# Up-projection of eight token tiles by seven products of half blocks

## The chip, the cores and the metric

The kernel runs on one core of a Trainium2 chip. The metric is the device time of one execution in microseconds (us); a kernel's time is the median of several executions. Engines are named as in the profile: PE is the matrix engine (PEld its weight loads), DVE is VectorE, ACT is ScalarE, POOL is GpSimd, SP is the engine that issues most transfers.

## The reference

A transformer block of 2048 tokens of width 640: linear attention with 32 heads behind a layer norm, then a feed-forward part behind another. Cut to what is computed:

```
def _A_ref(x, wqkv, w_phi, wo):                  # 32 heads of 20
    q, k, v = split_heads(x @ wqkv)
    pq, pk = q @ w_phi, k @ w_phi
    phi_q = concat(softmax(pq), softmax(-pq));  phi_k = concat(softmax(pk), softmax(-pk))
    kv = sum_s(phi_k v);  z = sum_s(phi_k)
    o = (phi_q kv) / (phi_q z + 1e-6)
    return o @ wo
def _B_ref(x, w1, w2):                           # w1 640 x 1728, w2 1728 x 640
    return silu(x @ w1) @ w2
h  = x + _A_ref(layernorm(x), wqkv, w_phi, wo)
h2 = h + _B_ref(layernorm(h), w1, w2)
```

## The kernel before

The 2048 tokens are 16 tiles of 128. Weights and activations stay in SBUF in bf16; PE writes into PSUM, 8 banks of 512 fp32 values per partition, and each result is taken out of its bank by ACT or DVE. The work of each tile goes through these steps, whose names are those of the order: keys and values (`K`, `V`, `ex`, `su`, `rk`, `sc`, `ve`, `kv`), queries (`Q`, `qe`, `qs`, `qr`, `qt`), attention (`D` on PE, `E` on DVE, `ot` a transposing transfer), output projection (`G{t}0`, `G{t}1` on PE, ten matmuls of 320 columns in all), residual (`ga`, DVE, line 856), second layer norm (`lm`, `ls`, `hn` on ACT, `lr` on POOL, `ht` a transposing transfer into `HnT`).

The feed-forward part works on units of tiles: (0, 1), (2 to 5), (6 to 9), (10 to 13), (14, 15). For a unit starting at tile a, the step `u{a}.{f}` makes one 128-wide block of the 1728 hidden columns (`ffn_up`, line 931): five matmuls, one for each 128-row chunk of the 640 inputs, that stream 512 columns (4 tiles) into one bank. There are 13 such blocks, f = 0 to 12, and `u{a}.L` makes the last 64 columns. `s{a}.{f}` is the SiLU on ACT (`ffn_silu`, line 954), from the bank into `shT`. In the units of two tiles a block streams 256 columns, and two blocks share a bank.

The down-projection already works on pairs of tiles by seven products of half blocks: `T1` to `T4` are sums of the halves of w2 on DVE (line 1001), `S1.t` to `S4.t` sums of the hidden rows (DVE, line 1018), `p1.t` to `p7.t` the products, seven matmuls of 320 columns each (line 1036), `r1`, `r2`, `r3`, `r7` take a bank with the residual into an fp32 tile (DVE, line 1044), and `w11` to `w22` add a bank to it and give the output rows (DVE, line 1051).

The order of all steps is written out by hand as one list, `ORDER`; each engine runs its own steps in the order of the list, and semaphores hold a step back until its inputs are there and its tile or bank is free. Banks are handed out by a ring (`ps_half`, `ps_two`): the next bank is the one handed out longest ago, and a matmul into it waits until its last reader has ended.

At the start PE runs matmuls of constants (`warm`), transposes the key weights (`wk`) and folds them (`fk{c}`, line 345), transposes the first normalised tiles (`xt`, line 530), and makes the first values chunk by chunk (`V0.{c}`, line 583) and the first keys (`K0.{c}`).

Of the kernel before, what the change touches and what calls it, by code (L numbers as in the profile page):

```python
# [27 lines left out]
ve9 sc5 xn12 kv5 sc6 rk7 ex8 wq5 st13 K9 fq5 sc7 ones6 ex9 load7 xt10 kv6 rs14 ref10 xn11 rs13 fq5e su8
Q0 kv7 st15 su9 eqr0 rk8 K10 qe0 V10 xn13 sc8 Q1 xn14 rs15 ex10 qs0 xt12 V12 kv8 ve10 rk9 sc9 ref13 qe1
su10 load9 ql0 ve12 load3 qs1 rk10 sc10 xt11 ref12 kv9 ref11 xt13 K12 xn15 K11 ex12 su12 K13 load1 ex11  # L30
ex13 load10 V11 kv10 xt14 su11 K14 ql1 load4 qi0 ve11 eqr1 V13 rk11 eqp su13 qi1 rk12 sc11 kv11 qr1
ref14 xt15 rk13 qr0 sc12 K15 ex14 su14 load0 Q2 ve13 kv12 sc13 ref15 ex15 rk14 su15 qe2 V14 rk15 V15
ve14 load5 Q3 kv13 sc14 mask1 kv14 ve15 sc15 qt1 qs2 load2 kv15 bd0 Q7 qt0 ql2 load6 load8 qi2 Q5 qe3
halves bd1 D0 D1 qr2 qe7 qe5 Q4 qs3 ql3 E0 Q10 E1 qi3 qr3 qs5 qe4 qe10 qt2 Q6 ql5 D2 ot0 qs4 qe6 ot1 Q9
qi5 ql4 qi4 qr5 qt3 qt5 E2 G00 qe9 G01 ga0 lm0 qr4 G11 ot2 G10 ls0 Q11 lr0 D3 qs6 qe11 Q8 ga1 E3 lm1 qt4
hn0 qs7 ot3 D5 E5 ls1 Q13 G20 qe8 lr1 ht0 G21 hn1 qe13 Q14 ht1 ga2 Q15 qr6 qs8 qe14 Q12 G31 qe15 qr7 D4
G30 qr8 E4 ot5 qt6 qe12 u0.L padL0 T3.0 u0.4 ga3 u0.6 qs9 s0.L G50 G51 D6 T1.1 T1.2 ga5 lm2 s0.4 s0.6
ls2 qt7 lm5 T2.2 u0.0 u0.8 s0.0 T3.2 ot4 s0.8 D7 lr2 lm3 E6 u0.12 ls5 qt8 u0.2 s0.2 padL1 E7 T4.2 S3.0
G41 ls3 T1.0 ot6 T3.1 lr5 G40 u0.10 D8 ga4 p7.0 T2.1 E8 G61 hn2 ot7 T2.0 lt0 hn5 lr3 lm4 s0.12 T4.1 G60
# [4 lines left out]
u2.11 qs14 E11 s2.8 s2.11 G90 S3.2 ls8 G91 D12 p7.2 qr14 G101 ga9 hn6 r7.2 S1.2 lm9 lr7 p1.2 qt13 ot11
D13 ls9 E12 S2.2 G100 lr9 lr8 hn7 p2.2 r1.2 qt14 p6.2 ga10 G110 w11.2 r2.2 p4.2 hn9 ht6 ot12 ht9 G111
ht7 E13 S3.4 D14 hn8 w21.2 S4.2 ga11 p5.2 w22.2 p7.4 lm11 ht8 r3.2 lm10 E14 ot13 ls10 S1.4 p1.4 r7.4
p3.2 r1.4 out0 S2.4 out1 G121 u6.L G120 p6.4 qs15 u6.8 ga12 G131 ot14 r2.4 p5.4 s6.8 qr15 lm12 ls11 G130
p4.4 w21.4 lr10 u6.12 ga13 out3 qt15 lr11 w22.4 out5 s6.12 u6.5 w12.2 G140 ls12 r3.4 D15 s6.L u6.4 lt6
hn10 lr12 ht10 hn11 G141 u6.0 ga14 E15 lm13 ls13 u6.11 s6.5 p2.4 s6.11 hn12 s6.4 u6.7 u6.10 u6.9 u6.2
s6.10 s6.2 u6.6 ot15 s6.0 s6.7 w11.4 lr13 G151 hn13 u6.3 s6.6 S4.4 ht11 ht12 s6.9 s6.3 G150 u6.1 ht13  # L50
p3.4 u10.L s6.1 S3.6 lm14 u10.7 ga15 u10.12 p7.6 s10.7 S3.8 S1.6 s10.L lt10 lm15 w12.4 ls14 u10.0 u10.2
p1.6 r1.6 u10.4 ls15 s10.2 out2 s10.12 u10.6 lr14 lr15 r7.6 hn15 hn14 S2.6 p6.6 S4.6 ht15 p2.6 s10.0
p4.6 r2.6 p3.6 p5.6 ht14 w21.6 u10.8 s10.4 r3.6 u10.3 u10.1 w22.6 w11.6 u14.L p7.8 s10.8 s10.3 w12.6
out4 s10.6 S1.8 r7.8 p1.8 u14.0 u10.10 u10.5 r1.8 s10.5 s14.L s10.1 out6 S2.8 p6.8 S4.8 u10.11 r2.8 p5.8
S3.10 u10.9 s10.9 p4.8 s10.11 w21.8 p2.8 u14.10 s14.0 w22.8 s10.10 r3.8 p3.8 p7.10 w11.8 u14.4 S1.10
u14.2 p2.10 p1.10 out7 S2.10 s14.2 w12.8 r7.10 s14.10 p4.10 u14.12 r1.10 p6.10 S4.10 u14.8 S3.12 s14.4
r2.10 w21.10 p5.10 S1.12 u14.6 p1.12 out9 w11.10 p3.10 S2.12 p2.12 r3.10 r1.12 s14.8 out8 w11.12 p6.12
p7.12 w22.10 r2.12 r7.12 s14.6 lt14 p5.12 S3.14 out11 S4.12 p1.14 s14.12 S1.14 p4.12 S2.14 r1.14 w12.10
w21.12 w22.12 p3.12 r3.12 p7.14 r7.14 p6.14 r2.14 S4.14 p4.14 w12.12 p5.14 out10 p3.14 p2.14 p2.14x
w21.14 w22.14 out13 out12 r3.14 out15 w12.14 w11.14 w11.14x out140 out141 out142  # L60
""".split()


# [1 line left out]
def kernel(  # L65
# [14 lines left out]
    T = 16  # L80
# [30 lines left out]
    keys = proj_ctx.enter_context(tc.tile_pool(name="keys", bufs=1, side="right"))  # L111
    proj = proj_ctx.enter_context(tc.tile_pool(name="proj", bufs=1, side="right"))
    fold_ctx = ctx.enter_context(ExitStack())
    early = fold_ctx.enter_context(tc.tile_pool(name="fold", bufs=1))
    pools = {"att": None, "late": None}

# [109 lines left out]
    def add(name, emit):  # L226
        steps[name] = emit
# [719 lines left out]
    def rows_of(u):  # L947
        if u not in shT:
            shT[u] = pools["late"].tile([P, 4 * FC * P], BF16, name="shT", bufs=NSH)
        return shT[u]  # L950

    def ffn_silu(u, f0, f1):
        n = (u[1] - u[0]) * P
        nc.scalar.activation(  # L954
            rows_of(u)[:, f0 * n : f1 * n], ps_of.pop(("u", u, f0))[:, 0 : (f1 - f0) * n], AF.Silu
        )

    SHL = {}
# [100 lines left out]
    for t in PAIRS:  # L1059
# [45 lines left out]

# [29 lines left out]
```

## Time and profile before

| | us |
|---|---|
| median of 3 executions | 225.18 (224.81 to 225.22) |
| profiled execution, its own time | 225.49 |
| its span in the profile | 223.8 |
| PE busy | 218.2 (98%) |
| DVE busy | 173.0 (77%) |
| ACT busy | 144.4 (65%) |
| POOL busy | 70.2 (31%) |
| granted PE clock, mean | 0.998 of full speed |

The profile gives for each engine the union of the times in which an instruction of it ran; "mean ns" is the duration of one instruction, which overlaps its neighbours. Times in the trace count from the start of the span; the execution's own time is 1.7 us longer than the span.

### The profile page before, as it was taken

Reading aid. Unit: us, or ns where it says so; the run is one execution under the profiler, and the core shown is the slowest. Engines: PE = TensorE matmul, PEld = TensorE weight load, DVE = VectorE, ACT = ScalarE, POOL = GpSimd, SP = SyncE. Lnnn points to the kernel's source line nnn. Section 1 sums busy time; section 2 is a strip of 40 time slices with the busy share of each in tenths; the row PEclk is TensorE's granted clock in tenths of the full one; section 3 lists DMA queues with packets and bytes.
Section 4 is the critical chain, followed back from the end, with each engine's and each line's share of the span. In section 5 each row is a group of like instructions: output and inputs, shape, how many; then the busy total and the mean of one; then the engine's idle time right before and its main releaser. Section 6 shows DMA issues by size and latency. Waiting matters only on the chain.

```text
span 223.8 us, 5031 instructions
## 1 busy us (share of the span) xinstructions
PE 218.2 (98%) x1926; PEld 154.8 (69%) x1935; DVE 173.0 (77%) x305; ACT 144.4 (65%) x321; POOL 70.2 (31%) x136
## 2 busy tenths in 40 slices
PE   8799999999999999999999999999999999999994
PEld 5677777777777777887655577665455656778773
DVE  4899999999989999999999999944024344436694
ACT  2799999999979899997086774268568332321000
POOL 6789899899000130163020130132004000000000
PEclk9999999999999999999999999999999999999999
DMA  6994639679999874935536666434512410010012
GB/s 174 320 263 134 114 77 165 185 190 161 315 201 175 175 134 81 213 56 107 126 78 139 126 145 124 120 95 81 63 29 53 91 60 0 29 44 0 29 62 88
DMA packets 68158, 26.98 MB, mean 121 GB/s; under 512 B 61159, under 2 KB 67111, under 8 KB 68007
## 3 DMA queue, kind: packets, MB, share of 16 engines
q1 hardware_dynamic: 67335, 26.61, 53.3%
q8 instruction: 15, 0.25, 0.5%
q10 hardware_dynamic: 800, 0.06, 0.3%
q14 instruction: 8, 0.07, 0.1%
HBM read 9.55 MB, written 2.62 MB: 54 GB/s over the span
## 4 chain that ended last, share of the span: by engine, by line
PE 94%; DMA 2%; SPq 2%; issue 0%; DVE 0%
PE banks L931 25%; PE banks L1036 24%; PE banks L571 18%; PE banks L849 10%; PE banks L609 9%; PE banks L817 3%; PE banks L662 2%; DMA Wv<-in_A_wqkv_dram 2%; PE banks L942 1%; SPq L181 1%; PE banks L583 1%; PE banks L437 1%; PE banks L598 1%; SPq L178 1%; PE banks L530 0%
## 5 line engine op out<-in xcount | busy, mean ns | idle before, releaser
L931 PE MATMUL banks<-HnT,w_sb 128*128 128x512 bf16 (+1 forms) x316 | 60.0, 335 | 0.4
L954 ACT ACTIVATE shT<-banks 128x512 bf16<-128x512 f32 (+1 forms) x53 | 29.1, 586 | 45.8 <-PE banks L931 44.8
L931 PEld LDWEIGHTS <-w_sb 128*128 128x128 bf16 x325 | 31.2, 98 | 21.2
L571 PEld LDWEIGHTS <-XnT 128*128 128x128 bf16 x300 | 28.5, 98 | 9.5
L494 POOL TENSOR_SCALAR xn<-X,mv,rs 128x640 bf16<-128x640 bf16 x12 | 30.6, 2550 | 1.7 <-ACT rs L485 1.4
L1036 PEld LDWEIGHTS <-S 128*128 128x128 bf16 x224 | 21.6, 98 | 8.8
L1044 DVE TENSOR_TENSOR r<-banks,X 128x320 f32<-128x320 f32 x32 | 15.4, 487 | 15.7 <-PE banks L1036 13.2
L516 POOL TENSOR_SCALAR rs<-mv 128x1 f32<-128x1 f32 x16 | 3.9, 244 | 73.8 <-ACT xn L509 73.5
L1036 PE MATMUL banks<-T,S 128*128 128x320 bf16 x168 | 26.1, 299 | 0.0
L849 PE MATMUL banks<-wo_sb,OT 128*128 128x320 bf16 x160 | 25.5, 299 | 0.1
L737 DVE TENSOR_REDUCE Sq<-EQ 128x66 f32<-128x1320 bf16 x16 | 24.2, 1519 | 0.0
L609 PE MATMUL banks<-Wfq,XnT 128*128 128x342 bf16 (+2 forms) x160 | 22.7, 293 | 0.0
L571 PE MATMUL banks<-Wv,XnT 128*128 128x320 bf16 x150 | 22.7, 299 | 0.0
L1051 DVE TENSOR_TENSOR o_t<-banks,r 128x320 bf16<-128x320 f32 (+2 forms) x33 | 14.9, 473 | 9.9 <-PE banks L1036 9.6
L630 DVE TENSOR_REDUCE Sk<-EK 128x64 f32<-128x1216 bf16 x16 | 22.2, 1403 | 0.1
L733 ACT ACTIVATE EQ<-banks 128x342 bf16<-128x342 f32 (+2 forms) x52 | 21.5, 526 | 0.4 <-PE banks L609 0.3
L1036 PEld LDWEIGHTS <-shT 128*128 128x128 bf16 x175 | 16.8, 98 | 6.6
L571 PE MATMUL banks<-Wfk,XnT 128*128 128x304 bf16 x150 | 21.3, 292 | 0.0
L626 ACT ACTIVATE EK<-banks 128x608 bf16<-128x608 f32 x32 | 20.3, 697 | 1.0 <-PE banks L571 0.5
L849 PEld LDWEIGHTS <-OT 128*128 128x128 bf16 x160 | 15.3, 98 | 6.7
L1018 DVE TENSOR_TENSOR S<-shT 128x896 bf16<-128x896 bf16 x16 | 9.8, 619 | 12.5 <-ACT shT L954 8.8
L609 PEld LDWEIGHTS <-XnT 128*128 128x128 bf16 x160 | 15.0, 97 | 5.4
(97 smaller groups left out, 329.2 us busy)
## 6 DMA issues: line engine op xcount, KB each, us to landing
out_dram<-o_t SPq DMA_DIRECT2D x15, 160.0 KB, 1.8
w_sb<-in_B_w_dram SPq DMA_DIRECT2D x5, 432.0 KB, 5.7
w_sb<-in_B_w_dram SPq DMA_DIRECT2D x3, 480.0 KB, 6.6
X<-in_A_x_dram SPq DMA_DIRECT2D x1, 1280.0 KB, 5.9
Wk<-in_A_wqkv_dram SPq DMA_DIRECT2D x5, 160.0 KB, 3.5
Wv<-in_A_wqkv_dram SPq DMA_DIRECT2D x5, 160.0 KB, 5.8
wo_sb<-in_A_wo_dram SPq DMA_DIRECT2D x1, 800.0 KB, 5.1
X<-in_A_x_dram SPq DMA_DIRECT2D x1, 640.0 KB, 6.5
```

The lines of the kernel that those rows point to most:

```text
L494: eng.tensor_scalar(out=xn_[t][:], in0=X[:, t, :], scalar1=mv_.pop(t)[:, 0:1], scalar2=rs_.pop(t)[:], op0=ALU.subtract, op1=ALU.mult,)
L571: nc.tensor.matmul(ps[:, g, 0:w], XnT[:, c, t * P : (t + 1) * P], W[:, c, g * w : (g + 1) * w], start=(c == 0), stop=(c == C - 1),)
L609: nc.tensor.matmul(ps[:, 0 : e - a], XnT[:, c, t * P : (t + 1) * P], Wfq[:, c, a:e], start=(c == 0), stop=(c == C - 1),)
L626: nc.scalar.activation(E5[:, :, :, b, 0:DR], p4, AF.Exp, scale=sign)
L630: nc.vector.tensor_reduce(sk[t][:], ek[t][:, 0 : H * HF].rearrange("p (q f) -> p q f", f=DH)[:, :, 0:DR], axis=AX.X, op=ALU.add)
L733: nc.scalar.activation(features(t, a, b)[:, :, :, i, 0:DR], p4, AF.Exp, scale=sign)
L737: nc.vector.tensor_reduce(sq[t][:], EQ[0][:, t, :, 0:FCH].rearrange("p c (q f) -> p c q f", f=DH), axis=AX.X, op=ALU.add)
L849: nc.tensor.matmul(ps_of["G", t][:, g, 0:HD], ot[t][:, c, :], wo_sb[:, c, g * HD : (g + 1) * HD], start=(c == 0), stop=(c == C - 1),)
L931: nc.tensor.matmul(ps[:, at : at + n], w1_sb[:, c, fc * P : fc * P + P], HnT[u][:, c, 0:n], start=(c == 0), stop=(c == C - 1),)
L954: nc.scalar.activation(rows_of(u)[:, f0 * n : f1 * n], ps_of.pop(("u", u, f0))[:, 0 : (f1 - f0) * n], AF.Silu)
L1036: nc.tensor.matmul(ps[:, lo:hi], left[:, c, :], right[:, c, lo:hi], start=(c == 0 and k in FIRST), stop=(c == KS - 1 and k in LAST), skip_ ...
L1044: nc.vector.tensor_tensor(r_[t, name][:], ps_of[bank, t][:, 0:HD], X[:, t + i, g * HD : (g + 1) * HD], op=ALU.add)
```

## The change

For the units of tiles 6 to 9 and 10 to 13 (`BYSUMS = (6, 10)`), the hidden blocks f = 0 to 11 are no longer made by `u{a}.{f}`. `u{a}.12`, `u{a}.L` and the other units stay as they were. Of the five input chunks the first four form a 2 by 2 scheme: w1 is cut into input halves (two chunks each) and column halves (768 columns each), the rows `HnT` into input halves and token halves (256 tokens each). For i = 0 to 5 the steps make block i and block i + 6 together. The fifth chunk is multiplied directly.

- `vw{k}.{part}` (DVE): four sums of w1's blocks, each in two parts of 128 x 2 x 384 bf16, made once; 8 steps.
- `vt{k}.{a}` (DVE): four sums of the rows' blocks, each 128 x 2 x 256 bf16; 4 steps for a unit.
- `vA` to `vE` (PE), for each unit and i: 4, 5, 2, 1 and 6 matmuls, all of 256 columns, into two banks. `vA` to `vD` write bank Y, `vE` bank X.
- `vc1` (ACT) copies all 512 columns of Y into an fp32 tile after `vA`; `vc2` and `vc3` copy 256 columns after `vB` and `vC`. `vB` waits for `vc1`, `vC` for `vc2`, `vD` for `vc3`, since each goes on adding in the bank that was read.
- `va0`, `va1` (DVE) add bank X and bank Y to the fp32 tile (512 columns each), `vs0`, `vs1` (ACT) are the SiLU from that tile into `shT`. The fp32 tile has two buffers, so that two i are in flight.

To make room, the buffer `EQ` of the query features is split in two, for tiles 0 to 8 and 9 to 15; the first is given up after the last of `qt0` to `qt8`, and the sums take its place. The whole list `ORDER` is another one: in the first steps (among others `fk4` and `xt1` now stand ahead of `V0.0`), in the middle, and from tile 6 on with the new steps. The diff, cut to its core:

```
+    TA = 9
+    def eq_at(t):
+        return EQ[t >= TA][:, t - TA * (t >= TA)]
...
     def pieces(u):
         m = 4 // (u[1] - u[0])
-        return [(f, min(f + m, FC - 1)) for f in range(0, FC - 1, m)]
+        begin = FC - 2 if u[0] in BYSUMS else 0
+        return [(f, min(f + m, FC - 1)) for f in range(begin, FC - 1, m)]
...
+    BYSUMS = (6, 10)
+    NF = (FC - 1) // 2 * P
+    def inner_weight_sum(k, part):
...
+        x, y, op = {
+            1: (a21, a22, ALU.add), 2: (SW.get(1), a11, ALU.subtract),
+            3: (a11, a21, ALU.subtract), 4: (a12, SW.get(2), ALU.subtract),
+        }[k]
+        at = slice(part * NF // 2, (part + 1) * NF // 2)
+        nc.vector.tensor_tensor(SW[k][:, :, at], x[:, :, at], y[:, :, at], op=op)
+    def row_sum(u, k):
...
+        x, y = {1: (b12, b11), 2: (b22, ST.get((u, 1))), 3: (b22, b12), 4: (b21, ST.get((u, 2)))}[k]
+        nc.vector.tensor_tensor(ST[u, k][:], x, y if k in (1, 3) else y[:], op=ALU.subtract)
+    def inner(u, i, which):
...
+        for bank, half, left, right, first, last in {
+            "A": (("Y", 1, a11, b11, 1, 0), ("Y", 0, SW.get(3), ST.get((u, 3)), 0, 0)),
+            "B": (
+                ("Y", 0, a22, ST.get((u, 4)), 0, 0), ("Y", 0, rest[1], rows[0], 0, 1),
+                ("Y", 1, SW.get(2), ST.get((u, 2)), 0, 0),
+            ),
+            "C": (("Y", 1, SW.get(1), ST.get((u, 1)), 0, 0),),
+            "D": (("Y", 1, rest[1], rows[1], 0, 1),),
+            "E": (
+                ("X", 0, a12, b21, 1, 0), ("X", 0, rest[0], rows[0], 0, 1),
+                ("X", 1, SW.get(4), b22, 0, 0), ("X", 1, rest[0], rows[1], 0, 1),
+            ),
+        }[which]:
...
+            m = 1 if left is rest[0] or left is rest[1] else 2
+            for c in range(m):
+                nc.tensor.matmul(
+                    ps, left[:, c, i * P : (i + 1) * P], right[:, c, :], start=bool(first) and c == 0,
+                    stop=bool(last) and c == m - 1, skip_group_check=True,
+                )
+    def inner_kept(u, i, which):
+        if which == 1:
+            vr_[u, i] = pools["sums"].tile([P, 4, n], F32, name="vr", bufs=2)
...
+        if which == 1:
+            act(r[:, 1:3], y)
+        else:
+            k = {2: 0, 3: 3}[which]
+            act(r[:, k : k + 1], y[:, 1:2])
+    def inner_added(u, i, j):
...
+        nc.vector.tensor_tensor(r, ps, r, op=ALU.add)
+    def inner_silu(u, i, j):
...
+        nc.scalar.activation(
+            rows_of(u)[:, f * n : (f + 1) * n].rearrange("p (b n) -> p b n", b=2),
+            vr_[u, i][:, 2 - 2 * j : 4 - 2 * j], AF.Silu,
+        )
```

The order at the start of unit 6, PE steps alone, before and after:

```
before: G121 u6.L G120 p6.4 u6.8 G131 p5.4 G130 p4.4 u6.12 u6.5 G140 D15 u6.4 G141 u6.0 u6.11 p2.4
after:  G121 G120 p7.4 u6.L p1.4 G131 G130 p6.4 p4.4 G140 vA.6.0 p5.4 vA.6.1 vB.6.0 G141 vC.6.0 vB.6.1
        D15 vE.6.1 vD.6.0 vE.6.0 vC.6.1 u6.12 vA.6.2 vD.6.1 p2.4 vB.6.2 vA.6.3 G151 vE.6.2 vC.6.2
```

More of the change, by code (lines that the diff above doesn't have):

```diff
@@ L44 @@
[L44 to L53, printed above, removed]
@@ new lines @@
+hn11 r2.4 vw3.0 vt3.6 vw1.0 out1 hn10 G140 vA.6.0 p5.4 vt2.6 w21.4 vt4.6 vc1.6.0 vw2.0 ga13 qt15 vA.6.1
+s6.L vc1.6.1 lr12 w22.4 vB.6.0 G141 vw4.0 vc2.6.0 vC.6.0 hn12 ht11 vc3.6.0 ga14 vB.6.1 D15 r3.4 vE.6.1
+vD.6.0 vE.6.0 E15 va1.6.0 ht10 vc2.6.1 vC.6.1 lm13 ls13 vc3.6.1 u6.12 vs1.6.0 va0.6.0 vA.6.2 vD.6.1 out0
+vs0.6.0 vc1.6.2 lr13 lt6 p2.4 s6.12 va0.6.1 va1.6.1 vw3.1 vs1.6.1 vw2.1 vs0.6.1 vB.6.2 ot15 vA.6.3 G151
+vw4.1 vc2.6.2 vc1.6.3 vE.6.2 vC.6.2 hn13 vc3.6.2 vB.6.3 G150 vD.6.2 vc2.6.3 w11.4 vA.6.4 va0.6.2 ht12
@@ new lines @@
+vC.6.3 va1.6.2 vE.6.3 vs0.6.2 vc3.6.3 ga15 vs1.6.2 vA.6.5 vD.6.3 vc1.6.4 ht13 vE.6.4 va0.6.3 vB.6.4
+vs0.6.3 va1.6.3 vs1.6.3 vc1.6.5 S4.4 vE.6.5 u10.L out3 vc2.6.4 vB.6.5 vC.6.4 lm15 vt3.10 u10.12 vc3.6.4
+vD.6.4 vc2.6.5 lm14 vC.6.5 vc3.6.5 va0.6.4 va1.6.4 vt1.10 out5 vE.10.0 vD.6.5 vs1.6.4 vs0.6.4 vA.10.0
+va1.6.5 vt2.10 s10.L s10.12 p3.4 vt4.10 out2 va0.6.5 vc1.10.0 vE.10.1 vA.10.1 vs0.6.5 vE.10.2 vs1.6.5
+S3.6 vB.10.0 p1.6 vc1.10.1 vc2.10.0 vC.10.0 ls14 vB.10.1 vc3.10.0 S1.6 r1.6 vc2.10.1 p7.6 lr14 S2.6
@@ new lines @@
+p4.8 r2.8 vc3.10.4 va0.10.4 vc1.10.5 vD.10.4 ht15 w21.8 w11.8 w12.6 vB.10.5 p5.8 out6 u14.L vc2.10.5
+va1.10.4 w22.8 u14.0 vC.10.5 vc3.10.5 r3.8 vE.10.5 vs0.10.4 u14.10 S4.8 s14.10 va0.10.5 s14.L lt14
+vD.10.5 p3.8 u14.6 vs1.10.4 va1.10.5 out7 vs0.10.5 u14.4 vs1.10.5 S3.10 s14.0 p7.10 s14.4 S3.12 u14.12
+p1.10 out9 p7.12 r1.10 u14.2 S1.10 w12.8 p2.10 S2.10 r7.10 S4.10 p6.10 p4.10 w11.10 r2.10 s14.6 w21.10
+p5.10 p1.12 s14.2 S1.12 r3.10 s14.12 w22.10 p3.10 S2.12 r7.12 w12.10 out10 r1.12 p2.12 p4.12 p6.12
@@ L113 @@
     fold_ctx = ctx.enter_context(ExitStack())
+    first_ctx = ctx.enter_context(ExitStack())
     early = fold_ctx.enter_context(tc.tile_pool(name="fold", bufs=1))
-    pools = {"att": None, "late": None}
+    pools = {"att": None, "late": None, "sums": None}
     banks = psum.tile([P, 8, 512], F32, name="banks")
```

138 lines of the change are left out of this document (97 added, 41 removed).

## The prediction

> **What bounds the kernel now.** I read the page first: busy shares, slices, chain.
>
> ```profile
> span 223.8 us, 5031 instructions
> PE 218.2 (98%) x1926; PEld 154.8 (69%) x1935; DVE 173.0 (77%) x305; ACT 144.4 (65%) x321; POOL 70.2 (31%) x136
> ...
> PE   8799999999999999999999999999999999999994
> PEld 5677777777777777887655577665455656778773
> DVE  4899999999989999999999999944024344436694
> ACT  2799999999979899997086774268568332321000
> ...
> PEclk9999999999999999999999999999999999999999
> ...
> PE 94%; DMA 2%; SPq 2%; issue 0%; DVE 0%
> ```
>
> PE has work nearly all the time, at full clock, and 94% of the chain that ended last is PE. So removed PE time comes off the end nearly one for one, as long as nothing else makes PE wait. DVE is as full as PE up to about slice 26 (145 us), then less than half used; ACT too has room after that. The changed steps run from about 145 us on. That is the room for what the change adds. Next, the windows of that stretch (from:to us, its length, then busy us and count of PE, PEld, DVE, ACT, POOL, then PE clock, DMA share, GB/s).
>
> ```profile
> 140.00:150.00 10.00, 9.95 (x82) 6.52 (x81) 7.42 (x15) 3.69 (x10) 2.14 (x6) 1.00 0.41 104
> 150.00:160.00 10.00, 9.95 (x63) 5.28 (x63) 3.18 (x6) 6.68 (x14) 2.08 (x6) 1.00 0.58 94
> 160.00:170.00 10.00, 9.89 (x73) 5.69 (x73) 2.04 (x4) 7.86 (x17) 0.23 (x1) 1.00 0.16 32
> 170.00:180.00 10.00, 9.95 (x62) 6.06 (x62) 4.57 (x10) 4.27 (x8) 2.13 (x6) 1.00 0.28 68
> 180.00:190.00 10.00, 9.95 (x69) 5.98 (x69) 4.72 (x10) 2.94 (x6) 0.00 (x0) 1.00 0.10 34
> 190.00:200.00 10.00, 10.00 (x79) 7.51 (x77) 3.82 (x8) 3.01 (x6) 0.00 (x0) 1.00 0.14 41
> ```
>
> **PE, removed and added.** The pace of matmuls is read from the chain (start us, us, what), not from their mean duration.
>
> ```profile
> 152.62 2.16 PE banks L931 x10
> ...
> 196.94 2.18 PE banks L931 x20
> ```
> ```profile
> L931 PE MATMUL banks<-HnT,w_sb 128*128 128x512 bf16 x186 | 44.4, 379 | 0.4
> ...
> L931 PE MATMUL banks<-HnT,w_sb 128*128 128x256 bf16 x130 | 15.8, 272 | 0.0
> ```
>
> At 512 columns one matmul takes 0.216 us, at 256 columns (unit 14) 0.109 us: half. Removed: 2 units x 12 blocks x 5 = 120 matmuls, 25.9 us. Added: 2 x 6 x (4+5+2+1+6) = 216 matmuls of 256 columns, 23.5 us. PE's work falls by 2.4 us. The saving is small because only four of five chunks go by seven products: 18 half-width matmuls for 20.
>
> The mean durations, 379 and 272 ns, would say the opposite: 120 x 0.379 = 45.5 us against 216 x 0.272 = 58.8 us. They contain the way through the array, 0.379 - 0.216 = 0.16 us, which overlaps the next matmul; I keep those 0.16 us as the price of a hand-over to another engine.
>
> The Trainium skill has a rule against this change: "TensorE: Matmul & The Clock Gate", "Back-to-back issue gap", gives some 131 ns for a 512-column matmul in a real stream and 81 ns for 128 columns. By it narrow matmuls are dear: a straight line between its figures gives, as an estimate, 98 ns at 256 columns, so 15.7 us removed for 21.2 us added, 5.5 us slower. The chain's 0.216 us contradicts the 131 ns.
>
> **ACT.** Added: 12 times one copy of 512 and two of 256 fp32 columns out of PSUM. The 24 SiLU stay, reading SBUF.
>
> ```profile
> L954 ACT ACTIVATE shT<-banks 128x512 bf16<-128x512 f32 x51 | 28.6, 595 | 45.8 <-PE banks L931 44.8 <-PE banks L1036 0.8
> ...
> L954 ACT ACTIVATE shT<-banks 128x256 bf16<-128x256 f32 x2 | 0.7, 370 | 0.0
> ```
> ```profile
> 160.08 1.57 ACT L954 ACTIVATE shT<-banks 128x512 bf16<-128x512 f32 x3 [1.56 <-PE banks L931]
> ```
>
> Three in a row take 1.57 us, so a queued one costs 0.52 us, 0.07 less than alone; 256 columns then cost 0.30. That is 0.52 + 2 x 0.30 = 1.12 us for each i, 6.7 us for a unit. From 140 to 170 us ACT had 3.69 + 6.68 + 7.86 = 18.2 of 30 us; with unit 6's copies 24.9. From 170 to 200: 10.2 + 6.7 = 16.9. It fits, tightest around 160.
>
> **DVE.** Added: 8 `vw` (768 bf16), 8 `vt` (512 bf16), 24 `va` (512 fp32, one input from a bank).
>
> ```profile
> L1044 DVE TENSOR_TENSOR r<-banks,X 128x320 f32<-128x320 f32 x32 | 15.4, 487 | 15.7 <-PE banks L1036 13.2 <-issue 2.3
> ...
> L856 DVE TENSOR_TENSOR X<-banks,X 128x640 bf16<-128x640 f32 x16 | 13.1, 816 | 2.8 <-PE banks L849 2.8
> ...
> L1001 DVE TENSOR_TENSOR T<-w_sb 128x640 bf16<-128x640 bf16 x4 | 1.8, 482 | 0.0
> ...
> L1001 DVE TENSOR_TENSOR T<-w_sb 128x960 bf16<-128x960 bf16 x2 | 1.3, 649 | 0.0
> ```
>
> From 320 to 640 fp32 columns the duration grows by 1.03 ns a column: 0.685 us at 512. From 640 to 960 bf16 columns by 0.52 ns: 0.55 us at 768, 0.415 at 512. Sum: 8 x 0.55 + 8 x 0.415 + 24 x 0.685 = 24.2 us, a tenth less where they queue (below). Of this 13.7 us are for unit 6 and the weights, `vw1.1` (0.55) of it already near 130 us, and 9.9 us for unit 10. From 140 to 170 us DVE had 12.6 of 30 us busy, with the additions 26; from 170 to 200, 13.1 + 9.9 = 23. It fits, but the first ones come while DVE is still full:
>
> ```profile
> 137.73 0.48 DVE L1051 TENSOR_TENSOR o_t<-banks,r 128x320 bf16<-128x320 f32 x1
> 138.13 0.48 DVE L1044 TENSOR_TENSOR r<-banks,X 128x320 f32<-128x320 f32 x1
> ...
> 144.73 0.50 DVE L768 TENSOR_TENSOR EQ<-EQ,Rho 128x660 bf16<-128x660 bf16 x1
> 147.70 0.49 DVE L1051 TENSOR_TENSOR o_t<-banks,r 128x320 bf16<-128x320 f32 x1 [2.47 <-PE banks L1036]
> ```
>
> And on PE, from the timeline `u6.12` with the block after it, and from the chain the pace of `G` (ten matmuls) and of the products (28):
>
> ```profile
> 147.50 2.32 PE L931 MATMUL banks<-HnT,w_sb 128*128 128x512 bf16 x10
> ```
> ```profile
> 101.27 1.36 PE banks L849 x10
> ...
> 105.88 3.80 PE banks L1036 x28
> ```
>
> The DVE row of 144.73 ends `qr15`, the last query step, at 145.23; the row after it has the first long DVE wait there. The first two rows show that queued ones start 0.40 us apart at 0.48 us each, so 0.08 overlaps. The second half of `vA.6.0` needs `vt3.6` and `vw3.0`. Up to `vt3.6` the new order has on DVE the steps up to `qr15` and besides them `vw1.1`, `vt1.6`, `vw3.0`, `vt3.6` and `w12.2` (0.48): 2.41 us less 5 x 0.08, ready at 147.2. On PE `u6.12` began at 147.50, right behind `p4.4`; ahead of `vA.6.0` stand the steps up to `p4.4` without `u6.8` (5 x 0.216 = 1.08) and `p5.4` (7 of 28 in 3.80: 0.95), with `G140` (5 of 10 in 1.36: 0.68) added. So PE is at `vA.6.0` at 146.15, at its second half at 146.37, and waits 0.8 us (0 to 1.2: DVE may hold small gaps that close). Behind it stand `p5.4`, `vA.6.1`, `vB.6.0`, which come later by the same.
>
> **Hand-overs.** `vA`, `vc1`, `vB`, `vc2`, `vC`, `vc3`, `vD` take turns on one bank. Where nothing covers a turn, PE loses 0.16 us until the result is there and the copy: 0.16 + 0.595 once and 0.16 + 0.37 twice, 1.8 us for each i, 22 us for twelve. The order puts other PE work in each turn: behind `vA.6.0` `p5.4` (0.95 us for a turn of 0.76), behind `vB.6.0` `G141` (0.68 for 0.53), behind `vC.6.0` `vB.6.1` (0.55), `D15` and `vE.6.1` (0.65) for 0.53 and `hn12`, which stands in ACT's queue ahead of `vc3.6.0`; behind `vA.6.2` `p2.4` (0.95), while `vs1.6.0` and `vs0.6.0` stand ahead of its copy on ACT. So single turns are covered with 0.15 to 0.2 us to spare, and those with other ACT work in front of the copy with hardly any. I take 0.4 us for twelve blocks, from 0 (all covered) to 2 (one turn in eleven bare).
>
> **The start.** In the timeline of the first microseconds PE stands still:
>
> ```profile
> 8.12 0.48 DVE L338 COPY WTk<-banks 128x640 bf16<-128x640 bf16 x1
> 8.51 0.43 DVE L494 TENSOR_SCALAR xn<-X,mv,rs 128x640 bf16<-128x640 bf16 x1
> ...
> 9.94 0.43 PE L583 MATMUL banks<-Wv,XnT 128*128 128x320 bf16 x2 [1.15 <-DMA Wv<-in_A_wqkv_dram]
> ```
> ```profile
> 10.37 0.38 PE banks L345 x6
> 10.75 0.28 PE banks L530 x5
> ```
>
> `fk4` (0.38) and `xt1` (0.28) now stand ahead of `V0.0`; their inputs are there at 8.60 and 8.94, and the queue of loads is the same up to this chunk. PE gets up to 0.66 us ahead. But DVE, full until 145 us, sets the pace at `vA.6.0`, and PE's lead turns into a longer wait there unless DVE's chain starts earlier too. I take 0.2 us of gain, 0 to 0.66.
>
> The rest of the new order holds the same work; `w12.2`, `G140` and such are moved past each other. I take nothing for it, 0.4 us either way, the spread of the three executions. The split of `EQ` adds two small memsets on POOL, which is 31% busy and not in the chain: at nothing.
>
> **Sum.** -2.4 (PE) + 0.8 (first sums) + 0.4 (hand-overs) - 0.2 (start) = -1.4 us. On the profiled execution's 225.5 this gives 224.1; the median of the runs is 0.3 lower, so 223.8 us.
>
> **The rivals.** About 0.2%, 0.45 us, is what a measurement of this kernel can tell from no change.
>
> First rival, slower: the turns on the bank are not covered. In place of the matmuls PE waits for ACT's copies, in unit 6 above all, where `lm`, `ls` and `hn` of tiles 12 to 15 stand in the same ACT queue. It decides from (1.4 + 0.4) / 22 = 8% of the turns' time on; at a fifth, 4.4 us in place of 0.4, the time is 227.8, at an eighth 226.2. For it: six dependent steps for 2 us of matmuls, and a bank that is held for several us in a ring that hands banks out in turn. Against it: PE waited only 0.05 to 0.1 us in each ten in these windows though each bank there, too, is read by ACT or DVE before it is used again. Chance 0.24.
>
> Second rival, no difference: DVE's lag at the start of unit 6 is not made up; `va` steps come late and keep banks, for another 1 us or so beside the 0.8. 225 us; chance 0.12.
>
> Third, that PE's pace at 256 columns is not half: then the change does not do what it says. The 2.18 us for 20 speak against it; by the mean durations it would be 13 us slower. I give 0.01, inside the slower side.
>
> The same page of the Trainium skill, "A second HAM failure mode: psum-queue depth-cycling", says that short stops between groups of matmuls can make the clock fall back and forth to half. Here PEclk stays at 9 in all slices, the one with the 1.15 us stop too. At half clock the new matmuls would cost another 23.5 us, 247 us in all. Chance 0.01, also inside the slower side.
>
> **Chances.** Forecast, 222.3 to 224.7: 0.62. Within 0.2%: 0.12. Slower: 0.26. With all waits at 0 and the start's gain whole the time would be 225.2 - 2.4 - 0.66 = 222.1; the fast end, 222.3, is just above, since not all of these come together. The slow end reaches into the first rival, 226.6, and leaves out some 0.1 beyond it.
>
> **What would show it.** Right: PE busy near 216 us; 216 matmuls of 256 columns at 0.109 us in the chain; DVE near 195, ACT near 158 us busy; one PE wait of some 0.8 us for DVE near 147 us, waits for ACT below 1 us in all; the first values begin after `fk4` and `xt1`, hardly any PE idle time before 10 us. Wrong: PE waits for ACT or DVE over 2 us in all between 145 and 190 us, copies above 0.6 us or `va` above 0.75 us, or a PE clock below full.

## The result, and the profile after

| | us |
|---|---|
| median before, 4 executions | 225.2 (224.81 to 225.61) |
| median after, 4 executions | 223.32 (223.29 to 223.32) |
| ratio | 0.9921, 95% interval 0.9905 to 0.9936 |
| forecast | 223.8 (222.3 to 226.6) |
| profiled execution after: own time, span | 223.32, 221.4 |

The kernel is 1.9 us faster by the medians; from one profiled execution to the other it is 2.17 us (225.49 to 223.32). In the trace PE is done 2.34 us earlier: the chain goes from PE to the last addition on DVE at 218.58 instead of 220.92. PE's end is read at this place in every kernel below.

The page of the changed kernel: span, busy times, slices, and the shares of the chain that ended last.

```profile
span 221.4 us, 5322 instructions
PE 217.1 (98%) x2031; PEld 164.5 (74%) x2031; DVE 194.0 (88%) x345; ACT 159.1 (72%) x357; POOL 71.6 (32%) x138
...
PE   8899999999999999999999999999999999999994
...
DVE  3999999999999999999999999999767984737874
ACT  2799999999879899998075785659899955451000
...
PEclk9999999999999999999999999999999999999999
...
PE 94%; DVE 3%; DMA 1%; POOL 0%; issue 0%; DVEq 0%
```

PE is still nearly the whole chain. DVE now stays full to about 155 us instead of 145 (a slice is 5.5 us), and ACT is nearly full from 149 to 177 us. The windows of the changed stretch (from:to us, its length, then busy us and count of PE, PEld, DVE, ACT, POOL, then PE clock, DMA share, GB/s) show what that costs PE:

```profile
140.00:150.00 10.00, 10.00 (x97) 7.76 (x95) 9.93 (x22) 6.09 (x12) 2.38 (x7) 1.00 0.52 118
150.00:160.00 10.00, 10.00 (x93) 8.11 (x92) 8.30 (x16) 9.39 (x21) 1.03 (x3) 1.00 0.35 72
160.00:170.00 10.00, 10.00 (x101) 8.25 (x100) 7.00 (x14) 9.57 (x23) 0.00 (x0) 1.00 0.13 46
170.00:180.00 10.00, 10.00 (x82) 7.87 (x81) 8.26 (x16) 8.37 (x19) 2.54 (x6) 1.00 0.20 46
180.00:190.00 10.00, 10.00 (x91) 8.03 (x90) 7.20 (x16) 4.92 (x10) 0.00 (x0) 1.00 0.10 22
190.00:200.00 10.00, 10.00 (x87) 8.29 (x86) 5.18 (x10) 4.79 (x10) 0.00 (x0) 1.00 0.17 53
```

It costs nothing: PE is busy for all 10.00 us of each window, though ACT is at 9.39 and 9.57 in two of them. Neither the 0.8 us wait for the first sums nor the hand-overs appear. (The 9.95 and 9.89 that the prediction shows for the kernel before are no stops: its page has 1926 matmuls for 1935 weight loads, and each of nine gaps of 0.05 us stands where one matmul has no record.) The groups by line of the changed kernel (partitions x elements, count, then busy us, mean ns of one, idle time ahead and what ended it):

```profile
L1032 PE MATMUL banks<-HnT,w_sb 128*128 128x256 bf16 x96 | 18.7, 273 | 0.0
...
L1053 DVE TENSOR_TENSOR vr<-banks,vr 128x512 f32<-128x512 f32 x24 | 16.3, 687 | 6.8 <-ACT vr L1047 4.0 <-PE banks L1032 2.6
L1058 ACT ACTIVATE shT<-vr 128x512 bf16<-128x512 f32 x24 | 14.5, 628 | 1.8 <-DVE vr L1053 1.6
L1047 ACT COPY vr<-banks 128x256 f32<-128x256 f32 x24 | 8.8, 371 | 6.1 <-PE banks L1032 5.7
L1044 ACT COPY vr<-banks 128x512 f32<-128x512 f32 x12 | 7.0, 588 | 3.2 <-PE banks L1032 2.9
```

The copies (588 and 371 ns) and the fp32 sums (687 ns) take what was forecast; the waits in these rows are ACT's and DVE's for PE, which cost nothing. The chain (start us, us, what) gives PE's pace at 256 columns and the end:

```profile
158.44 3.82 PE banks L1032 x35
...
209.97 8.59 PE banks L1141 x70
218.56 0.02 issue
218.58 0.29 DVE o_t L1156
```

3.82 us for 35 matmuls is 0.109 us for one, as forecast, where their mean duration is 273 ns.

### The profile page after: what moved, and what is told of

Its sections match the earlier page's. It is cut to its first block, busy times and chain, and to the rows that moved or that the text cites. A ratio compares the mean times of both kernels' runs of the same rounds, so it can differ in the third digit from the quotient of the medians.

```text
span 221.4 us, 5322 instructions
## 1 busy us (share of the span) xinstructions
PE 217.1 (98%) x2031; PEld 164.5 (74%) x2031; DVE 194.0 (88%) x345; ACT 159.1 (72%) x357; POOL 71.6 (32%) x138
## 4 chain that ended last, share of the span: by engine, by line
PE 94%; DVE 3%; DMA 1%; POOL 0%; issue 0%; DVEq 0%
PE banks L1141 24%; PE banks L593 18%; PE banks L954 14%; PE banks L1032 11%; PE banks L871 10%; PE banks L631 9%; PE banks L839 3%; PE banks L684 2%; DMA WPH<-in_A_w_phi_dram 1%; PE banks L965 1%; DVE st L500 1%; PE banks L448 1%; PE banks L605 1%; PE banks L620 1%; DVE xn L516 1%; PE banks L552 0%
## 5 line engine op out<-in xcount | busy, mean ns | idle before, releaser
L954 PE MATMUL banks<-HnT,w_sb 128*128 128x256 bf16 (+1 forms) x205 | 33.1, 312 | 0.0
L977 ACT ACTIVATE shT<-banks 128x512 bf16<-128x512 f32 (+1 forms) x29 | 15.9, 580 | 23.6 <-PE banks L954 23.6
L516 POOL TENSOR_SCALAR xn<-X,mv,rs 128x640 bf16<-128x640 bf16 x12 | 30.0, 2504 | 1.4 <-ACT rs L507 1.2
L954 PEld LDWEIGHTS <-w_sb 128*128 128x128 bf16 x205 | 19.6, 98 | 8.8
L1053 DVE TENSOR_TENSOR vr<-banks,vr 128x512 f32<-128x512 f32 x24 | 16.3, 687 | 6.8 <-ACT vr L1047 4.0
L1032 PE MATMUL banks<-HnT,w_sb 128*128 128x256 bf16 x96 | 18.7, 273 | 0.0
L1141 PE MATMUL banks<-w_sb,shT 128*128 128x320 bf16 (+2 forms) x119 | 17.7, 291 | 0.0
L548 ACT ACTIVATE xn<-X,rs 128x640 bf16<-128x640 bf16 x16 | 14.5, 918 | 2.4 <-POOL rs L542 2.4
```

The source lines that it names most:

```text
L516: eng.tensor_scalar(out=xn_[t][:], in0=X[:, t, :], scalar1=mv_.pop(t)[:, 0:1], scalar2=rs_.pop(t)[:], op0=ALU.subtract, op1=ALU.mult,)
L954: nc.tensor.matmul(ps[:, at : at + n], w1_sb[:, c, fc * P : fc * P + P], HnT[u][:, c, 0:n], start=(c == 0), stop=(c == C - 1),)
L977: nc.scalar.activation(rows_of(u)[:, f0 * n : f1 * n], ps_of.pop(("u", u, f0))[:, 0 : (f1 - f0) * n], AF.Silu)
L1032: nc.tensor.matmul(ps, left[:, c, i * P : (i + 1) * P], right[:, c, :], start=bool(first) and c == 0, stop=bool(last) and c == m - 1, skip ...
L1053: nc.vector.tensor_tensor(r, ps, r, op=ALU.add)
L1141: nc.tensor.matmul(ps[:, lo:hi], left[:, c, :], right[:, c, lo:hi], start=(c == 0 and k in FIRST), stop=(c == KS - 1 and k in LAST), skip_ ...
```

## The experiments

The theory: the time goes with PE's matmul time (some 1.2 us for each unit), VectorE's and ScalarE's additional work lies beside PE, and the order covers the turns on the bank. The rivals: the new order itself is the gain; the additional work costs something that the saving hides; the turns would not cost much without the order. Each kernel below is the changed one with one edit. The ratios are to the kernel before on the same chip (medians 225.03 to 225.17 us there), with their 95% intervals. First the changed kernel once more, unedited:

> The changed kernel once more, unchanged, for comparing the start variants on the same chip: 223.3 us within 0.2.

223.42 us (223.34 to 223.44), ratio 0.992 (0.9906 to 0.9933): the same as the first time.

**The new order without the products.** `BYSUMS` empty; the direct blocks take the places of `vA` and `vE`, their SiLU one PE step behind.

```
- BYSUMS = (6, 10)
+ BYSUMS = ()
  ORDER:  vA.{a}.{i} -> u{a}.{i+6}   vE.{a}.{i} -> u{a}.{i}   vB vC vD vc va vw vt left out
```

> The order of the changed kernel, but both units by five matmuls a block as before: block f = i in the place of vE, f = i + 6 in the place of vA, each SiLU one PE step behind its block, no sums and no copies. Theory (the whole gain is PE work saved by the products, 120 x 0.216 less 216 x 0.109 = 2.3 us): 223.3 + 2.3 = 225.6 us, the time of before within 0.4. Rival (the new order of the other steps gave a good part, over 0.8 us): 224.8 or less.

226.43 us (226.16 to 227.98), ratio 1.0075 (1.0044 to 1.0106). The windows of this kernel in which PE stops:

```profile
170.00:180.00 10.00, 9.78 (x60) 5.56 (x59) 3.87 (x8) 4.81 (x9) 2.92 (x6) 1.00 0.16 39
...
190.00:200.00 10.00, 9.87 (x87) 7.67 (x86) 3.87 (x9) 2.94 (x6) 0.00 (x0) 1.00 0.20 53
```

The end of its chain:

```profile
221.62 0.29 DVE o_t L1146
```

PE ends at 221.62, 3.04 us behind the changed kernel. The two stops show as 0.22 and 0.13 us of idle time; each is 0.16 us longer than that, because the records draw out a matmul's end by that much (0.379 - 0.216 us in the prediction); 0.67 us together. In the first PE waits for a sum of hidden rows on DVE, which I put down to the places that I gave the blocks; for the second, at a block of `u14`, the profile names no cause on PE. They account for most of the 0.8 us by which the time is above my expectation. What is left of the 3.04 us, 2.4, is the PE work that the products save. The order alone gains nothing: against the kernel before, this one ends 0.70 us later, and 0.67 us of that are its two stops. The rival that the order is the gain falls.

**One unit of two.** `BYSUMS = (6,)`; unit 10 as in the experiment above.

```
- BYSUMS = (6, 10)
+ BYSUMS = (6,)
```

> As the changed kernel, but tiles 10 to 13 by five matmuls a block; tiles 6 to 9 keep the products and all sums of w1 are made. Theory (each unit saves the same PE work): 223.3 + 1.15 = 224.5 us. Rival (unit 6, which comes while VectorE is full, gives its saving back, and unit 10 brings all): 225.5 us. Rival (unit 10 brings nothing): 223.3 us.

225.17 us (224.90 to 225.27), ratio 1.0004 (0.9994 to 1.0013). PE ends at 220.37: 1.25 us ahead of the kernel without products, and 1.79 us behind the changed one, of which 0.62 us are the same two stops (0.17 and 0.13 us, each and 0.16). The time is 0.7 us above my expectation, most of it by these stops. So unit 6 gives 1.25 us and unit 10 gives 1.17, each near the forecast 1.2 (the first with 0.05 us of the stops in it).

**No sums of blocks on DVE.** In `inner` single blocks of w1 and of the rows stand where `vw` and `vt` would have left sums, so the hidden rows of tiles 6 to 13 are others than the reference's; the matmuls are as many and as large.

```
+ SW = {1: a21, 2: a22, 3: a11, 4: a12}
+ ST = {(u, 1): b12, (u, 2): b22, (u, 3): b11, (u, 4): b21}
  ORDER:  the 16 steps vw, vt left out
```

> As the changed kernel, but without the sums of w1 and of the rows (16 steps of VectorE, 6.7 us queued): the products read single blocks of w1 and of the rows instead, so the output is another. Theory (PE waits for none of the sums): 223.3 us within 0.2, and no change in the PE windows. Rival (the sums hold PE somewhere, hidden in the way that ends of matmuls are modelled): faster by 0.3 us or more.

223.41 us (223.38 to 223.49), ratio 0.9929 (0.991 to 0.9948): no difference from the changed kernel. One window of this kernel, to set beside the same window above:

```profile
140.00:150.00 10.00, 10.00 (x96) 7.74 (x94) 7.13 (x14) 6.05 (x12) 2.19 (x7) 1.00 0.52 117
```

DVE has 2.8 us less to do there (7.13 for 9.93), and PE gains nothing. The sums lie wholly beside PE's work.

**More sums ahead of the first products.** Four more sums of the kind of `vw` (into a part of `SW4` that is written again later) ahead of `vt1.6` on DVE. It measures how much room there is at `vA.6.0`.

```
+ for i in range(4):
+     add(f"xx{i}", ...)   # nc.vector.tensor_tensor(SW[4][:, :, at], a21[:, :, at], a22[:, :, at], op=ALU.add)
  ORDER:  xx0 xx1 xx2 xx3 ahead of vt1.6
```

> As the changed kernel, with four more sums of w1 (128 x 768 bf16, about 0.47 us each when queued, 1.9 us in all) on VectorE just ahead of vt1.6; their result is written over later. Theory (VectorE sets when vA.6.0 can run, 0.36 us to spare as vt3.6 ended at 145.99 and PE came to its second half at 146.35; beyond that a wait of PE lands at the end one for one): PE waits 1.5 us near 147 us, 224.8 us. Rival (VectorE makes the lateness up in the gaps that its queue still has behind, and the order gives PE other work): under 223.8 us.

225.49 us (225.40 to 226.73), ratio 1.0026 (1.0011 to 1.0042). First the changed kernel's timeline around `vA.6.0` (start us, us, engine, line, operation), then this kernel's:

```profile
145.57 0.42 DVE L1007 TENSOR_TENSOR ST<-HnT 128x512 bf16<-128x512 bf16 x1
...
146.13 0.38 PE L1032 MATMUL banks<-HnT,w_sb 128*128 128x256 bf16 x2
146.35 0.38 PE L1032 MATMUL banks<-ST,SW 128*128 128x256 bf16 x2
```
```profile
144.28 2.33 DVE L1004 TENSOR_TENSOR SW<-w_sb 128x768 bf16<-128x768 bf16 x4
...
147.73 0.42 DVE L1017 TENSOR_TENSOR ST<-HnT 128x512 bf16<-128x512 bf16 x1
...
148.20 0.38 PE L1042 MATMUL banks<-ST,SW 128*128 128x256 bf16 x2 [1.70 <-DVE ST L1017]
```

In the changed kernel `vt3.6` ends at 145.99 and the second half of `vA.6.0`, which needs it, begins at 146.35: 0.36 us of room. Here `vt3.6` is 2.16 us later, and PE's second half 1.85 us; PE's end is 2.02 us later (220.60). So lateness beyond the 0.36 us, 1.80 us here, comes through to the end in full. The four sums took 2.33 us, 0.56 to 0.58 each, not the 0.47 that I had counted for queued ones: the result is 0.7 us above my expectation, of which 4 x 0.1 us is that, and the rest is not taken apart.

**More work on ACT.** The SiLU `vs0` done twice, into the same place: 12 more activations.

```
  def inner_silu(u, i, j):
+     for _ in range(2 - j):
          nc.scalar.activation(...)
```

> As the changed kernel, with vs0 done twice in each i: 12 more activations of 512 columns from SBUF, 0.53 us each when queued, 6.4 us in all, 3.2 of them in unit 6, where ScalarE was 95% busy (1.0 us free in 150 to 170 us). Theory (PE runs with ScalarE's queue just covered there): ScalarE lacks about 2 us in unit 6, PE waits for copies by 1 to 2 us there and hardly in unit 10: 224.3 to 225.3 us. Rival (ScalarE's queue is not what covers PE, the lateness stays off the path): 223.3 to 223.6 us.

227.22 us (227.18 to 227.23), ratio 1.0096 (1.0078 to 1.0115); PE ends at 222.46, 3.9 us behind the changed kernel, for 6.4 us of work. One window and two rows of the timeline of this kernel:

```profile
170.00:180.00 10.00, 8.98 (x73) 6.88 (x72) 6.97 (x14) 9.87 (x22) 2.09 (x6) 1.00 0.12 31
```
```profile
155.04 0.38 PE L1032 MATMUL banks<-ST,w_sb 128*128 128x256 bf16 x2 [0.37 <-ACT vr L1044]
...
173.49 0.38 PE L1032 MATMUL banks<-ST,SW 128*128 128x256 bf16 x2 [0.91 <-ACT vr L1047]
```

The waits that the profile names are for `vc1` (L1044), three times in unit 6, 1.0 us in all, and for `vc2` (L1047) once in unit 10, 0.91 us; shorter stops in both units have no name there. My expectation was low by 2 to 3 us, since it had hardly a wait in unit 10. ACT's queue is the next bound: of 6.4 us more it hid 2.5.

**The turns uncovered.** In unit 6 the steps of each i stand back to back in the list, `vE` first, with no other PE work between them.

```
  ORDER, unit 6, for each i:  vE vA vc1 vB vc2 vC vc3 vD
```

> As the changed kernel, but in tiles 6 to 9 the steps of one i stand right behind each other on PE (vE vA vB vC vD), so that nothing covers the turns on the bank; the same work. Theory (each uncovered turn costs PE the way of the result, 0.16 us, and the copy, 0.59 or 0.37): 1.8 us for each i, 6 of them, 223.3 + 10.9 = 234.2 us, with PE waits for ScalarE of that sum; up to 2 us more where lm, ls or hn stand ahead of a copy in ScalarE's queue. Rival (the turns are cheaper, since the next product's weights are loaded meanwhile and ScalarE is quicker when idle): under 229 us.

240.52 us (239.73 to 241.15), ratio 1.0686 (1.0649 to 1.0722). The first three turns in the timeline of this kernel, with what PE waited for, and its waits for the copies in all (us in total, times, longest; one of the 19, 0.30 us, is in unit 10):

```profile
150.63 0.59 ACT L1044 COPY vr<-banks 128x512 f32<-128x512 f32 x1 [4.66 <-PE banks L1032]
...
151.27 0.38 PE L1032 MATMUL banks<-ST,w_sb 128*128 128x256 bf16 x2 [0.67 <-ACT vr L1044]
...
152.43 0.38 PE L1032 MATMUL banks<-ST,SW 128*128 128x256 bf16 x2 [0.46 <-ACT vr L1047]
...
153.27 0.27 PE L1032 MATMUL banks<-HnT,w_sb 128*128 128x256 bf16 x1 [0.46 <-ACT vr L1047]
```
```profile
PE banks L1032 <- ACT vr L1047: 5.5, 12, 0.5
PE banks L1032 <- ACT vr L1044: 4.9, 7, 1.1
```

The matmuls of `vA` follow one another until 150.43, so its turn to 151.27 costs 0.84 us; those of `vB` and `vC` cost 0.62 each. That is 2.08 us for one i where I had 1.82. The 18 waits of unit 6, each longer by 0.16 us than it shows, come to 13 us for six i. What the cover of one unit is worth is thus 13 us, against 1.25 us that its products save. The remaining 4 of the 17 us are other waits of PE, ahead of these (0.86 us of idle time at 148.79) and behind, and its clock; this run does not divide them. The windows of this kernel:

```profile
160.00:170.00 10.00, 6.33 (x55) 4.65 (x53) 4.34 (x9) 5.53 (x12) 0.00 (x0) 0.96 0.23 66
170.00:180.00 10.00, 7.45 (x57) 5.04 (x56) 2.46 (x5) 4.55 (x10) 0.00 (x0) 0.87 0.00 0
```

After 18 us of such stops the granted clock fell: a finer window shows 0.50 from 169.17 to 172.58 us, and 1.00 on both sides of it, though the stops go on to 181 us; the 0.96 and 0.87 are the means of the windows that this stretch lies in. The Trainium skill, "TensorE: Matmul & The Clock Gate", "A second HAM failure mode: psum-queue depth-cycling", says that frequent short stops of PE between groups of matmuls, from cycling through PSUM, make the clock go back and forth. This trace agrees with one fall and return, 3.4 us long; that the stops caused it is not shown. In the changed kernel, without the stops, it is 1.00 in every window above.

**A third unit.** `BYSUMS = (2, 6, 10)`, with an order for unit 2 that I placed by hand. This order lets a bank be written again before its reader has run, so the hidden rows of unit 2 are not the reference's.

> The products for tiles 2 to 5 as well (BYSUMS = (2, 6, 10)), the sums of w1 made ahead of them, the new steps put by hand into the places of u2.0 to u2.11. PE work falls by another 1.15 us. Theory (VectorE is as full as PE up to 145 us, so the 8.7 us of sums and additions of this unit, and 4 us of sums of w1 that now come earlier, make PE wait): 6 to 12 us slower than the changed kernel, 229 to 235 us, with PE waits for VectorE or for banks that VectorE still holds between 110 and 150 us. Rival (PE has other work meanwhile and the time is given back after 145 us, where VectorE has room): under 225 us.

244.34 us (244.11 to 245.24), ratio 1.0857 (1.0836 to 1.0879). A window and two groups of waits of this kernel:

```profile
120.00:130.00 10.00, 5.05 (x23) 2.48 (x22) 8.41 (x15) 3.51 (x8) 0.00 (x0) 0.68 0.34 72
```
```profile
PE banks L1037 <- DVE ST L1012: 2.9, 1, 2.9
...
PE banks L876 <- DVE vr L1058: 3.7, 1, 3.7
```

PE waits for DVE (row sums, and the sums that free its banks) and its clock falls to 0.68. Which part is DVE's lack of room, which is the bare turns of my order and which the clock, this run does not separate; whether a third unit could pay stays open.

**The first steps.** My forecast had up to 0.66 us from `fk4` and `xt1` ahead of `V0.0`. Four kernels change only the first steps of the order. First, up to `K0.3` as in the kernel before:

```
  ORDER:  up to K0.3 as before the change; then the changed order
```

> As the changed kernel, but with the first steps, up to K0.3, in the order of before. The first keys began at 11.30 us before and at 11.43 after. Theory (PE sets the end from then on): 223.3 - 0.1 = 223.2 us. Rival (VectorE, full from 10 to 145 us, takes any lead of PE away): 223.3 us or, if VectorE starts later, up to 0.3 more.

222.84 us (222.33 to 223.89), ratio 0.9903 (0.9873 to 0.9934). Second, the same with `fk4` and `xt1` (and what they need, `fk0e` and `xn1`) ahead of `V0.0`:

```
  ORDER:  ... fk0e fk4 xn1 xt1 V0.0 ...
```

> As the run with the first steps in the order of before, but with fk0e, fk4, xn1 and xt1 ahead of V0.0, so that fk4 and xt1 (0.38 + 0.28 us) run while PE waits for the first chunk of the value weights. Theory (PE's lead of 0.66 us lasts to the end, VectorE follows by closing its gaps): 223.3 - 0.1 - 0.66 = 222.5 us. Rival (VectorE's pace up to 146 us takes the lead away, all but the 0.36 us to spare at vA.6.0): 222.9 to 223.3 us, with a PE wait for VectorE between 20 and 147 us.

222.75 us (222.59 to 223.01), ratio 0.9899 (0.9879 to 0.9919). The first keys (`K0`) start at 10.50 in this kernel's timeline, and at 11.27 in the changed kernel's. Then most of the lead is lost:

```profile
10.50 1.46 PE L620 MATMUL banks<-Wfk,XnT 128*128 128x304 bf16 x10
...
12.49 0.89 DVE L500 BATCH_NORM_STATS2 st<-X 128x6 f32<-128x320 bf16 x2 [1.21 <-DMA X<-in_A_x_dram]
...
13.99 0.45 PE L552 MATMUL banks<-ident,xn 128*128 128x128 bf16 x5 [0.47 <-DVE xn L516]
```

`st4` waits on DVE for a load of X that has not landed, `xn2` stands behind it, and PE waits for `xn2`. So, third, `st4` behind `xn2`, and `rs2` ahead of two other steps on POOL:

```
  ORDER:  as above, and  ... xn2 st4 ...   ... st2 rs2 ...   (mask0 and own then behind rs2)
```

> As the run with fk4 and xt1 moved ahead of V0.0, but with st4 (which waits for the fourth load of x) behind xn2 on VectorE, and rs2 ahead of mask0 and own on GpSimd. In that run PE stood still before xt2, at 13.99 us, since xn2 stood behind st4. Theory (PE's lead lasts once it is there; only this wait took it away): xt2 about 0.6 us earlier, 222.75 - 0.5 = 222.2 us. Rival (VectorE, full up to 145 us, gives no more than the lead seen so far): 222.7 us, with a PE wait for VectorE later on.

225.28 us (224.92 to 225.72), ratio 1.0005 (0.9995 to 1.0016), a miss by 3 us. POOL in this kernel's timeline:

```profile
10.86 0.22 POOL L509 TENSOR_SCALAR rs<-mv 128x1 f32<-128x1 f32 x1 [3.37 <-DVE mv L501]
...
13.99 5.02 POOL L516 TENSOR_SCALAR xn<-X,mv,rs 128x640 bf16<-128x640 bf16 x2
```

`rs2` now waits at the head of POOL's queue for 3.37 us, and everything behind it is late, with `xn3` and `xn4` only from 13.99 on; PE then stops for `xt3` and again near 27 us. Fourth, `st4` behind `xn2` alone:

```
  ORDER:  as the second, and  ... xn2 st4 ...
```

> As the run with fk4 and xt1 moved ahead of V0.0, with st4 behind xn2 on VectorE and nothing moved on GpSimd. In the run that moved rs2 too, rs2 waited 3.4 us on GpSimd for its moments with mask0, own and xn3 queued behind it, and PE then waited for xn3. Theory (PE's lead lasts to the end once these waits are gone): xt2 at 13.4 us, no wait before xt3, 222.2 us. Rival (VectorE, full up to 145 us, gives no more lead): 222.7 us.

222.62 us (222.19 to 222.86), ratio 0.9881 (0.9863 to 0.9899). This is the fastest version, 2.5 us below the kernel before, and its interval lies below that of the changed kernel (0.9906 to 0.9933). The time alone is nearer my rival's 222.7 than the 222.2 of the theory; the trace decides between them. In this kernel's timeline and its chain:

```profile
10.46 1.46 PE L620 MATMUL banks<-Wfk,XnT 128*128 128x304 bf16 x10
...
14.46 0.97 PE L593 MATMUL banks<-Wv,XnT 128*128 128x320 bf16 x6 [0.15 <-DMA Wv<-in_A_wqkv_dram]
```
```profile
67.99 0.71 PE banks L839 x24
...
209.48 8.59 PE banks L1141 x70
```

`K0` is 0.81 us ahead of the changed kernel's; the stop for a load of `Wv` costs 0.31 (0.15 seen, 0.16 drawn out); the lead of 0.49 us at 67.99 (68.48 there) is 0.49 us still in the last 70 matmuls (209.48 for 209.97). PE has no wait for DVE in this kernel: its lead at the start is not taken back by DVE. How the lead divides between the four kernels is less sure: those with before's first steps wait for loads there, and their executions spread by 0.4 to 1.6 us, where the changed kernel's, which waits for `xn1` on DVE instead, spread by 0.1 us at most.

## Why the prediction was right, point by point

**What bounds it, and PE's work (-2.4).** Right: -2.34 us at PE's end, and the kernel without products, without its own two stops, is 2.4 us slower. In the chains of the two profiled executions the same step starts at 68.50 before and 68.48 after, so the 2.34 us arise behind it. The pace at 256 columns was 0.109 us. The straight line through the Trainium skill's figures on the page "TensorE: Matmul & The Clock Gate" ("Back-to-back issue gap") had, as an estimate, 5.5 us slower; the trace contradicts it after the change as before, with the 0.109 us.

**The first sums (+0.8).** This is the term that was mis-sized: it was 0. PE reached the second half of `vA.6.0` at 146.35, as forecast (146.37), but `vt3.6` ended at 145.99, not 147.2. The step that failed was to take DVE's time ahead of it as fixed, with each added step pushed behind the others. In fact `qr15` ended earlier than before with more work ahead of it, as the rows of the two timelines show (the first of the changed kernel; that of before, 144.73, stands in the prediction):

```profile
143.88 0.50 DVE L790 TENSOR_TENSOR EQb<-EQb,Rho 128x660 bf16<-128x660 bf16 x1
```

The sum lines of the windows from 60 to 140 us, first of the kernel before, then of the changed one:

```profile
sum 80.00, PE 79.84 PEld 57.58 DVE 76.69 ACT 61.40 POOL 14.56; mean PE 9.98 PEld 7.20 DVE 9.59 ACT 7.68 POOL 1.82
```
```profile
sum 80.00, PE 80.00 PEld 57.61 DVE 77.95 ACT 62.20 POOL 16.03; mean PE 10.00 PEld 7.20 DVE 9.74 ACT 7.77 POOL 2.00
```

DVE was busy for 77.95 of the 80 us, where it had been 76.69: nearly full is not full, and 1.3 us of small gaps closed. The 16 products that scale the key features also took 827 ns each instead of 863, but nine of those that scale the query features took 548 instead of 498, so that the two nearly cancel; why, no run shows. The prediction's bracket (0 to 1.2, "small gaps that close") held the answer at its end. That it was close is shown by the four extra sums: a little over 0.36 us more and PE would have waited. (The prediction's 13.7 us of DVE work for unit 6 and the weights leaves out `vw1.1`; with it, it is 14.3.)

**The hand-overs (+0.4).** Measured 0: no window from 140 to 200 us has PE below 10.00. Stops under 0.16 us each would not show there, but the saved work of 2.4 us came whole, which leaves them no room. The covers that the prediction named are what does it: uncovered, the turns cost 2.08 us for each i (forecast 1.8) and 13 us in one unit. The prediction's argument that PE waited 0.05 to 0.1 us in each ten before rested on the missing records; PE did not wait at all there. The first rival was thus real in its mechanism and price, and did not occur in this order.

**The start (-0.2).** Wrong in sign, though small: `K0` began at 11.27 where it had been 11.14 in the timeline of before. `fk4` and `xt1` went ahead of `V0.0`, but the inputs of `xt1` came later than the 8.94 us that I had read, since the steps of DVE ahead of it had been moved too. The changed kernel's timeline:

```profile
3.50 0.51 DVE L316 TENSOR_TENSOR WPD<-WPH 128x95 bf16<-128x95 bf16 x1 [3.50 <-DMA WPH<-in_A_w_phi_dram]
...
9.58 0.79 DVE L516 TENSOR_SCALAR xn<-X,mv,rs 128x640 bf16<-128x640 bf16 x1
```

DVE's first step now waits for the transfer of the feature weights, and `xn1` is done at 10.37. With the first steps as before, `K0` starts at 10.57 us and PE ends 0.36 us earlier without the move of `fk4` and `xt1` (218.22); with it, and `st4` behind `xn2`, `K0` starts at 10.46 and PE ends 0.49 us earlier (218.09). So the assumption that DVE takes PE's lead back was wrong too. Nor is the 1.15 us stop for `Wv` that I read in the trace of before a fixed price: in the kernel with before's first steps, PE did not stop there. By the medians that kernel is 2.33 us below the one before on the same chip (222.84 and 225.17), about the 2.4 of PE work, and the changed kernel 1.9; so its new first steps lost some 0.5 us, as far as the spread of 1.6 us there allows to say.

**Second rival, DVE's lag is not made up.** Did not occur; leaving all 16 sums out changes nothing.

**Third rival, pace; and the clock.** Neither occurred in the changed kernel. The clock fell in the kernel with uncovered turns and in the one with three units.

**The engines.** PE 217.1 us busy (near 216 forecast), DVE 194.0 (195), ACT 159.1 (158). PE's busy time fell by 1.1 us alone, because 1.2 us of its idle time went as well: 0.75 in the first 20 us, and the nine gaps of missing records. From 140 to 170 us ACT had 6.09 + 9.39 + 9.57 = 25.0 us where 24.9 was forecast.

**The sum.** -1.4 forecast, -2.17 measured between the profiled executions; the gap of 0.77 us is the wait (0.8) and the hand-overs (0.4) that did not come, less the start (0.2) that did not come either, and 0.23 us by which the time fell short of the forecast 2.4 us of PE work; 0.17 of these lie outside PE's end (2.34) and are not explained. I had then taken off 0.3 us because the profiled execution of before was above its median; that of after stands at its median, so this step took back part of the error, and 223.8 lay 0.5 us above the measured 223.32. The mechanism was right; that the number came so near, with three terms off, is in part luck.

## What to carry to other kernels

Where one engine is the chain, cost a change by that engine's pace in a row (0.109 us), not by mean durations (273 ns), and then look for the one place where another engine is full when the new work arrives: here 0.36 us of room decided whether the gain came whole. A scheme that reads a bank between its own matmuls lives from the other work put into each turn; without it one unit lost ten times what its products saved, and for 3.4 us PE had half its clock as well. Before counting on an input's time, check that the steps ahead of it on its own engine are the same in the new order.

## What the runs showed of the hardware

- A turn on one bank, matmul to ACT's copy and back to the next matmul, cost 0.84 us at 512 columns and 0.62 us at 256: the copy (0.59, 0.37) and 0.25 us.
- Stops of PE of 0.6 to 1.3 us, mostly after 0.2 to 1 us of matmuls, were followed after 18 us by a granted clock of 0.50 for 3.4 us (0.96 and 0.87 as means of 10 us), and by 1.00 again while they went on. Four stops of at most 0.91 us of idle time between 155 and 174 us, with twice the SiLU `vs0`, left it at 1.00.
- SiLU of 512 fp32 values took 628 ns when it read SBUF, 595 ns when it read a bank (`vs` against `s`).
- Four sums into the same tile in a row on DVE took 2.33 us for 0.55 us each alone: they did not overlap, where rows of different tiles overlapped by some 0.08 us.
